# Attention and a two-layer SiLU network on one core: attention sums in sixes and sevens, layer-1 chunks evicted in pairs, and TensorE's order as a table

## The chip, the cores and the metric

The kernel runs on one core of a Trainium2 chip. The metric is the device time of one execution in microseconds (us). The engines are called by the profile's names: PE is TensorE (PEld its weight loads), DVE is VectorE, ACT is ScalarE, POOL is GpSimd, SP is SyncE.

## The reference

```python
# q, k, v: [8 batches, 8 heads, 576 positions, 64], x 0.1
scores = q @ k.T / 8                              # per batch and head
mask_plain = (rel >= 0) & (rel < 32)              # heads 0 to 3, rel = query - key
mask_dil = (rel >= 0) & (rel < 128) & (rel % 4 == 0)   # heads 4 to 7
attn = softmax(where(mask, scores, -1e9)) @ v
x = attn.transpose(0, 2, 1, 3).reshape(4608, 512)
h = x @ w_in                                      # [512, 2048]
out = (h * sigmoid(h)) @ w_out                    # [2048, 512], float32
```

## The kernel before

**Attention, batch by batch.** The four plain heads are cut into six blocks of 96 queries (`QB`), each with 128 keys. The four dilated heads are cut by residue (position modulo 4, `DIL`) into four sequences of 144, and each of these into two halves of 72 (`MH`). A batch goes through these steps: for batches 0 to 2, transposes of k and q on PE (`TA`, `TB`, `TS` plain; `TD`, `TR` dilated), for batches 3 to 7 DMA transposes instead; `S`, six or seven score tiles, with an exponential on ACT (L701 and L705) and, behind batch 0, a mask product on DVE (L711); `V`, a copy of the dilated values (`vd_of`); `P` and `D`, the attention sums (`av`, L735); `XP` and `XD`, transposes of the sums into the input `xA` of layer 1 (batches 0 to 4; batches 5 to 7, `BYDMA`, store to DRAM in `x_s` and come back by DMA transposes).

In `av` four matmuls, one per head, each write 65 columns of one PSUM bank: 64 sums and, in the last, the sum of the weights. DVE then takes the reciprocal of the four weight sums (L741) and multiplies (L742) into `oP` or `oD`. There are six `P` and eight `D` steps in a batch, 14 in all, with 4 x 64 columns each.

**The two layers, by groups of tokens.** `GROUPS` are two groups of 256 tokens (0 and 1) and eight of 512 (2 to 9). Layer 1 (`l1`, L970) makes one chunk of 128 hidden columns with four matmuls into a bank `h`. ACT applies SiLU directly (L984), or, while its tables are those of the exponential, Tanh into `th` (L987), after which DVE finishes with `(th + 1) * h` (L989); both write `gT`. Groups 8 and 9 (`FAST1`, `l1_fast`, L1077 onwards) multiply by the scheme of Strassen and Winograd with seven products of half size. Layer 2 is plain for groups 0 and 1 (L1129) and uses seven products for groups 2 to 9 (`layer2_fast`, L1209), in two blocks a group. It needs sums of `gT` blocks (`g_sums`, L1165, on DVE; group 8 on POOL). Its results leave PSUM by ACT (L1229, L1239) and DVE (L1236) into `ob`, and the store of `ob` is issued on ACT's queue, from group 7 on SP's. `ob` has two buffers.

**PSUM.** Eight banks: `h` two, `y` and `u` for layer 2, `x` and `z` for attention's small tiles and, in groups 0, 1, 8 and 9, for layer 1, and two for scores (`s`). Scores can also take the pairs `hh` or `xz`.

**What sets the order.** The kernel writes each engine's instructions out itself. A planner (`Plan`) holds a clock, the time at which each engine is free, and estimated costs. Each piece of work is a `Step` whose generator issues its matmuls first and then says which engine it uses for how long; `ANY` lets the planner choose ACT or DVE by which would end first. At every turn the loop at the end of the kernel makes a list of candidates, from the attention steps `att` (at most `LOOK` ahead), layer 1 (`l1`, in order, or `LOOK1` ahead in groups 8 and 9), layer 2 (`l2`) and the block sums (`sums`), and starts the first that is ready in planned time and whose engine has no more than a limit of backlog:

```python
cands = main + cands if side > SIDE else cands + main
...
    r = max(r, plan.t + plan.backlog(it[1].uses) - lim)
    if r <= plan.t:
        pick = q_, it
```

The order within attention is the list `order` in `attention(b)`, one for batch 0, one for batches 1 and 2, one for the rest. On the chip each engine works through its own list in order and waits on semaphores, and nothing of the planner's clock remains.

Of the kernel before, what the change touches and what calls it, by code (L numbers as in the profile page):

```python
# [10 lines left out]
F32 = mybir.dt.float32  # L11
# [5 lines left out]
def kernel(  # L17
# [43 lines left out]
    LOOK1 = 6  # L61
# [36 lines left out]
    oD = cpool.tile([MH, 2, DIL, HN, D], F16, name="oD")  # L98
    rcps = cpool.tile([P, NB + 2 * DIL, HN], F32, name="rcps")
# [166 lines left out]
    for t in probs:  # L266
        c = 2 * 4 * MH
        n = PW + P - c
        nc.scalar.copy(t[:, c:], vraws[1].rearrange("p a h r d -> p (a h r d)")[:, :n])
# [46 lines left out]
    HOP = 0.18  # L316
# [3 lines left out]
    LEAN = 0.1  # L320
    ORD = 1

    class Step:
        def __init__(self, make, pe, rings=(), deps=(), uses=()):
            self.make, self.pe, self.rings, self.deps, self.uses = make, pe, rings, deps, uses
            self.after = self.keep = self.done = self.mate = self.behind = None
            self.started = False
            self.freed = None
            self.mode = 128

    class Plan:
# [13 lines left out]
        def push(self, step, gen, ready, value=None):  # L345
            self.now = ready
            try:
# [3 lines left out]
                return  # L351
            heapq.heappush(self.heap, (ready, self.n, step, gen, eng, us))
            self.n += 1

        def flush(self):
            while self.heap and self.heap[0][0] <= self.t:
# [9 lines left out]
                if eng in ("EXP", "L1", "SILU"):  # L366
                    mode = "silu" if eng == "SILU" else "exp"
                    if eng == "L1" and (self.table == "silu" or not self.soon()):
                        mode = "silu"
                    if mode == "silu" or eng == "EXP":  # L370
# [3 lines left out]
                if eng == "ANY":  # L374
                    ends = {e: max(ready, self.free[e]) + n for e, n in us.items()}
                    eng = min(ends, key=ends.get)
# [153 lines left out]
    def attention(b):  # L530
# [204 lines left out]
        def av(ring, key, o, rcp, lhs, rhs):  # L735
            a = small(ring, [P, HN, 66], F32, f"av_{b}_{key}")
            for i in range(HN):
                nc.tensor.matmul(a[:, i, : D + 1], lhs(i), rhs(i), start=True, stop=True)  # L738
            n = o.shape[0]
            yield "DVE", 0.545  # L740
            nc.vector.reciprocal(rcp[:n], a[:n, :, D : D + 1])  # L741
            nc.vector.tensor_tensor(  # L742
                o, a[:n, :, :D], rcp[:n, :, None].broadcast_to([n, HN, D]), ALU.mult
            )

        def av_p(ring, j):
            def lhs(i):
                return prob_cols(("p", j, i // 2), i % 2)

            yield from av(  # L750
                ring, f"p{j}", oP[:, j], rcps[:, j], lhs, lambda i: vp[:, i * NB + j, : D + 1]
            )
            parts[j // 3] += 1
            if b in BYDMA and parts[j // 3] == 3:
                j = j // 3 * 3
# [7 lines left out]
                x_stored(b, j // 3)  # L763

        def av_d(ring, ab, r):
            def lhs(i):
                return prob_cols(("d", ab, r // 2, i), r % 2)

            yield from av(
                ring, f"d{ab}{r}", oD[:, ab, r], rcps[:, NB + ab * DIL + r], lhs,  # L770
                lambda i: vd[:, ab, i, r, : D + 1],
            )
            parts[2 + ab] += 1
            if b in BYDMA and parts[2 + ab] == DIL:
                r0 = BYDMA.index(b) * S + ab * DIL * MH
                rows = x_s[r0 : r0 + DIL * MH, HN * D :].rearrange("(m r) c -> m r c", r=DIL)
                nc.sync.dma_start(out=rows, in_=oD[:, ab].rearrange("p r h d -> p r (h d)"))
                yield "DMA", 3.0
                x_stored(b, ab)
# [32 lines left out]
        if b == 0:  # L812
            order = [
                ("TA", 1, "q"), ("TA", 0, "q"), ("V", 0), ("TD", 3), ("TS", 1), ("TS", 0),
                ("TD", 0), ("TA", 0, "k"), ("TD", 2), ("TD", 1), ("TA", 1, "k"), ("S", 3),
                ("TR",), ("S", 4), ("S", 6), ("S", 0), ("S", 1), ("D", 0, 1), ("P", 1), ("S", 5),
                ("D", 0, 0), ("D", 0, 2), ("V", 1), ("P", 0), ("S", 2), ("P", 3), ("P", 2),
                ("D", 1, 1), ("P", 4), ("D", 0, 3), ("P", 5), ("XP", 0), ("XP", 1), ("D", 1, 2),
                ("XD", 0), ("D", 1, 0), ("XP", 4), ("D", 1, 3), ("XP", 5), ("XP", 2), ("XD", 1),
                ("XP", 3), ("M",), ("B",),  # L820
            ]
        elif b < ORD:
            order = [
                ("N", "k"), ("TD", 3), ("TD", 0), ("TD", 2), ("V", 0), ("TD", 1), ("N", "rest"),
                ("TA", 1), ("N", "q"), ("S", 3), ("TA", 0), ("TB", 0), ("TB", 1), ("D", 0, 1),
                ("D", 0, 0), ("S", 4), ("D", 0, 2), ("S", 0), ("P", 1), ("S", 1), ("D", 0, 3),
                ("P", 2), ("P", 0), ("XP", 0), ("XP", 1), ("S", 5), ("S", 6), ("XD", 0), ("V", 1),
                ("D", 1, 3), ("XP", 2), ("S", 2), ("D", 1, 2), ("D", 1, 0), ("D", 1, 1), ("P", 3),
                ("XP", 3), ("P", 4), ("XD", 1), ("P", 5), ("XP", 4), ("XP", 5),
            ]  # L830
        elif pe_path:
            order = [
                ("N", "k"), ("TD", 3), ("TD", 0), ("TD", 2), ("V", 0), ("TD", 1), ("N", "rest"),
                ("TA", 1), ("N", "q"), ("TA", 0), ("TB", 0), ("TB", 1), ("S", 3), ("S", 4),
                ("S", 0), ("S", 1), ("S", 5), ("S", 6), ("S", 2), ("D", 0, 1),
                ("D", 0, 0), ("D", 0, 2), ("P", 1), ("D", 0, 3),
                ("P", 2), ("P", 0), ("XP", 0), ("XP", 1), ("XD", 0), ("V", 1),
                ("D", 1, 3), ("XP", 2), ("D", 1, 2), ("D", 1, 0), ("D", 1, 1), ("P", 3),
                ("XP", 3), ("P", 4), ("XD", 1), ("P", 5), ("XP", 4), ("XP", 5),
            ]  # L840
        else:
            order = [
                ("S", 0), ("S", 1), ("S", 2), ("S", 3), ("S", 4), ("S", 5), ("P", 1), ("P", 0),
                ("V", 0), ("P", 2), ("D", 0, 0), ("XP", 0), ("V", 1), ("D", 0, 1), ("XP", 1), ("D", 0, 2),
                ("D", 0, 3), ("XP", 2), ("P", 3), ("P", 4), ("XD", 0), ("P", 5), ("D", 1, 0),
                ("XP", 3), ("D", 1, 1), ("XP", 4), ("D", 1, 2), ("D", 1, 3), ("XP", 5), ("XD", 1),
# [3 lines left out]
        for key in order:  # L850
            kind, a = key[0], key[1:]
            rings = ["x", "z"] + (["h", "y", "u"] if b == 0 else ["h"] if b < 2 else [])
# [48 lines left out]
            elif kind == "P":  # L901
                us = sorted({home["p", a[0], hp][0] for hp in range(HP // 2)})
                st = Step(
                    lambda ring, a=a: av_p(ring, *a), 0.13, rings,
                    [AT_VP1 if b == 0 and a[0] > 2 else at_vp] + [steps["S", u] for u in us],
                    ("DVE",),
                )
            elif kind == "D":
                us = sorted({home["d", a[0], a[1] // 2, h][0] for h in range(HN)})
                st = Step(  # L910
                    lambda ring, a=a: av_d(ring, *a), 0.13, rings,
                    [steps["V", a[0]]] + [steps["S", u] for u in us], ("DVE",),
                )
            elif kind == "XP":
                st = Step(lambda ring, a=a: x_p(ring, *a), 0.1, rings, [steps["P", a[0]]], x_eng)
            else:
                st = Step(
                    lambda ring, a=a: x_d(ring, *a), 0.28, rings,
                    [steps["D", a[0], r] for r in range(DIL)], x_eng,
# [16 lines left out]
            if kind in "PD":  # L936
# [3 lines left out]
                if 3 <= b + 2 < B:  # L940
                    st.after = lambda: count(
                        ("V", b), NB + 2 * DIL,
# [24 lines left out]
    def layer1(g, deps):  # L967
        w = GROUPS[g][1]

# [27 lines left out]
        queue, even, odd = [], [], []  # L997
# [421 lines left out]
```

## Time and profile before

| | |
|---|---|
| runs shown | 303.99, 305.06, 305.07 us, median 305.06 |
| profiled execution | 305.17 us, its span in the profile 303.4 us |
| granted TensorE clock | 0.989 of full speed, at half from about 7.5 to 14.3 us |
| PE, DVE, ACT, POOL busy | 288.5, 215.2, 194.6, 97.9 us |
| layer 1 (L975), layer 2 (L1209), groups 8 and 9 (L1077), plain layer 2 (L1129) | 27%, 27%, 8%, 4% of the chain that ended last |

The shares of busy time are averages over stages with different limits: attention of batches 0 to 2 with its transposes lies before about 80 us, layers 1 and 2 with the attention of batches 3 to 7 from there to 230 us, and the seven-product layers alone behind that. Rows of the windows give busy times by stage, rows of the timeline give start and length and, in brackets, how long the engine had been idle and what released it. A matmul's row reaches to the modelled end of its results, while the next matmul can start before that.

### The profile page before, as it was taken

How to read it: one execution, taken by the hardware profiler on the slowest of the kernel's cores; microseconds unless marked ns; L12 is line 12 of the kernel's file. 1: busy time of each engine (PE TensorE's matmuls, PEld its weight loads, DVE VectorE, ACT ScalarE, POOL GpSimd, SP SyncE). 2: the span in 40 equal slices, each digit the busy share in tenths (PEclk: the TensorE clock that was granted, in tenths of full speed). 3: DMA queues.
4: the chain of work that ended last, by engine and by line, in shares of the span. 5: the costliest groups of instructions: out<-in, count | busy, mean ns of one | idle time of the engine just before them, and what ended most of it. 6: DMA issues, size and time to landing. Idle time of an engine off the chain costs nothing.

```text
span 303.4 us, 7434 instructions
## 1 busy us (share of the span) xinstructions
PE 288.5 (95%) x2922; PEld 203.0 (67%) x2922; DVE 215.2 (71%) x598; ACT 194.6 (64%) x427; POOL 97.9 (32%) x135
## 2 busy tenths in 40 slices
PE   6779999989999999999989999999999999999995
PEld 2458765644567666666765577558647888888884
DVE  6288999889958785768654788476767686599511
ACT  7477784378687766766746675667665496388320
POOL 8764824000740060005000659700700069800000
PEclk9599999999999999999999999999999999999999
DMA  7999999999899989989958999943114401200231
GB/s 97 180 199 198 197 194 201 208 186 194 94 155 171 240 101 182 214 179 118 210 128 182 158 192 264 211 84 110 47 34 108 110 2 50 90 2 0 86 124 71
DMA packets 100106, 42.26 MB, mean 139 GB/s; under 512 B 68584, under 2 KB 95464, under 8 KB 100072
## 3 DMA queue, kind: packets, MB, share of 16 engines
q0 software_dynamic: 48528, 19.86, 54.2%
q1 hardware_dynamic: 48088, 15.64, 26.0%
q10 hardware_dynamic: 3456, 6.29, 6.2%
q8 instruction: 23, 0.38, 0.5%
q14 instruction: 11, 0.09, 0.1%
HBM read 39.81 MB, written 17.10 MB: 188 GB/s over the span
## 4 chain that ended last, share of the span: by engine, by line
PE 77%; DVE 11%; DMA 6%; ACT 3%; issue 1%; POOL 1%; ACTq 0%; DVEq 0%; POOLq 0%
PE h L975 27%; PE y L1209 27%; PE h L1077 8%; PE y L1129 4%; DMA out_dram<-ob 4%; PE av_d L738 2%; PE s L692 2%; DMA nat<-in_q_dram 2%; DVE gT L989 2%; PE av_p L738 1%; DVE probs L711 1%; DVE oD L742 1%; DVE ob L1236 1%; DVE oP L742 1%; PE xp L784 1%
## 5 line engine op out<-in xcount | busy, mean ns | idle before, releaser
L975 PE MATMUL h<-xA,w_in 128*128 128x512 f16 (+1 forms) x512 | 110.4, 352 | 1.8 <-ACT probs L705 0.9
L984 ACT ACTIVATE gT<-h 128x512 f16<-128x512 f32 x84 | 49.6, 597 | 29.0 <-PE h L975 28.6
L975 PEld LDWEIGHTS <-w_in 128*128 128x128 f16 x512 | 45.2, 97 | 32.6 <-issue 2.5
L1209 PEld LDWEIGHTS <-gT 128*128 128x128 f16 x512 | 49.0, 98 | 8.6 <-issue 1.6
L1209 PE MATMUL y<-w_out,gT 128*128 128x256 f16 x384 | 48.4, 273 | 0.1
L1209 PEld LDWEIGHTS <-work 128*128 128x128 f16 x384 | 37.0, 98 | 7.0 <-issue 1.1
L1236 DVE TENSOR_TENSOR ob<-y,nat 128x256 f32<-128x256 f32 x48 | 20.1, 422 | 25.4 <-PE y L1209 23.3
L512 POOL COPY fence<-kqT 128x1 f16<-128x1 f16 x10 | 3.9, 397 | 94.8 <-DMA kqT<-kq_s 94.8
L1209 PE MATMUL y<-w_sum,work 128*128 128x256 f16 x256 | 32.0, 273 | 0.4 <-ACT nat L1229 0.4
L738 PEld LDWEIGHTS <-probs 128*128 128x128 f16 x448 | 22.9, 98 | 13.0 <-DVE oP L742 1.7
L701 ACT ACTIVATE probs<-s 128x768 f16<-128x768 f32 (+2 forms) x31 | 24.5, 791 | 6.3 <-PE s L692 3.4
L742 DVE TENSOR_TENSOR oD<-av_d,rcps 72x256 f16<-72x256 f32 x64 | 26.9, 421 | 2.2
L1229 ACT COPY nat<-y 128x256 f32<-128x256 f32 x48 | 17.9, 384 | 10.7 <-PE y L1209 9.5
L987 ACT ACTIVATE th<-h 128x256 f32<-128x256 f32 (+1 forms) x44 | 19.2, 445 | 7.3 <-PE h L975 4.7
L989 DVE SCALAR_TENSOR_TENSOR gT<-th,h 128x256 f16<-128x256 f32 (+1 forms) x44 | 20.6, 487 | 2.2 <-ACT th L987 2.1
L741 DVE RECIPROCAL rcps<-av_d 72x4 f32<-72x4 f32 x64 | 11.1, 173 | 14.9 <-PE av_d L738 14.8
L1239 ACT COPY ob<-y 128x256 f32<-128x256 f32 x16 | 5.9, 371 | 24.2 <-PE y L1209 21.6
L705 ACT ACTIVATE probs<-s 128x288 f16<-128x288 f32 (+2 forms) x40 | 18.5, 485 | 4.6 <-ACT ob L1239 1.4
L742 DVE TENSOR_TENSOR oP<-av_p,rcps 96x256 f16<-96x256 f32 x48 | 20.2, 421 | 1.6
L711 DVE TENSOR_TENSOR probs<-probs,mask_p 128x768 f16<-128x768 f16 x21 | 12.2, 584 | 10.2 <-ACT probs L701 7.4
L1209 PE MATMUL y<-w_sum,gT 128*128 128x256 f16 x128 | 16.6, 272 | 1.0 <-DVE ob L1236 1.0
L738 PE MATMUL av_d<-vd,probs 128*128 128x65 f16 x256 | 16.5, 194 | 0.6 <-ACT probs L705 0.3
(129 smaller groups left out, 484.3 us busy)
## 6 DMA issues: line engine op xcount, KB each, us to landing
out_dram<-ob ACTq DMA_DIRECT2D x24, 256.0 KB, 4.0
out_dram<-ob SPq DMA_DIRECT2D x12, 256.0 KB, 2.0
kq_s<-in_k_dram POOLq DMA_DIRECT2D x5, 576.0 KB, 9.1
kq_s<-in_q_dram POOLq DMA_DIRECT2D x5, 576.0 KB, 12.9
vp<-in_v_dram POOLq DMA_DIRECT2D x7, 384.0 KB, 7.0
w_out<-in_moe_w_out_dram POOLq DMA_DIRECT2D x4, 512.0 KB, 10.9
vraw<-in_v_dram POOLq DMA_DIRECT2D x8, 224.0 KB, 5.4
w_in<-in_moe_w_in_dram POOLq DMA_DIRECT2D x3, 512.0 KB, 9.5
```

What stands on the lines that cost most here:

```text
L701: nc.scalar.activation(p2, both[:, :, :n], AF.Exp, scale=scale)
L705: nc.scalar.activation(p2[:, i], sp[i][:, :n], AF.Exp, scale=scale)
L738: nc.tensor.matmul(a[:, i, : D + 1], lhs(i), rhs(i), start=True, stop=True)
L742: nc.vector.tensor_tensor(o, a[:n, :, :D], rcp[:n, :, None].broadcast_to([n, HN, D]), ALU.mult)
L975: nc.tensor.matmul(h[:, :w], w_in16[:, c, f * P : (f + 1) * P], x_g[:, c], start=(c == 0), stop=(c == HP - 1),)
L984: nc.scalar.activation(gTs[g][:, f, :w], h[:, :w], AF.Silu, scale=2.0)
L987: nc.scalar.activation(th[:, :w], h[:, :w], AF.Tanh)
L989: nc.vector.scalar_tensor_tensor(gTs[g][:, f, :w], th[:, :w], 1.0, h[:, :w], ALU.add, ALU.mult)
L1077: nc.tensor.matmul(y, lhs[:, c, j], rhs[:, c], start=first and c == 0, stop=c == 1, skip_group_check=not first,)
L1209: nc.tensor.matmul(y, lhs[:, c, tb * P : (tb + 1) * P], rhs[:, c], start=first and c == 0, stop=c == KP - 1, skip_group_check=not first,)
L1229: nc.scalar.copy((t1, t5, u2)[n], y)
L1236: nc.vector.tensor_tensor(half, y, (u2, t5, t1)[n - 3], ALU.add)
```

## The change

It has three parts.

1. **Attention sums.** The 24 plain sums of a batch (6 blocks x 4 heads) and the 32 dilated sums (2 halves x 4 residues x 4 heads) are counted through in one row each. `RUN_P` and `RUN_D` cut them into runs of six, and of seven, seven, six, six and six, and each run fills one bank of up to 7 x 66 columns with one reciprocal and one multiply. `P` has four steps, `D` five. `XP` j waits for the runs that hold its four sums, `XD` for three runs; a run can span two blocks or both halves.
2. **Layer 1 of groups 0 and 1.** `l1_two` makes two chunks of 256 columns in one bank and evicts both with one SiLU, or one Tanh and one product.
3. **The order.** The candidates loop is replaced by a table: `SEQ` names, start by start, the queue (`a` attention, `l` layer 1, `y` layer 2, `s` sums) and the place in it. Steps without matmuls start as soon as their inputs are there in planned time (`early`). `CHOICE` fixes the engine of some copies and SiLU or Tanh for some chunks, and `SHIFT` moves the planned time of some steps, which changes where their instructions stand on ACT and DVE. `HOP` goes from 0.18 to 0.16 and `LEAN` from 0.1 to 0.05, `FAST1`'s look-ahead `LOOK1` is gone, the lists `order` are rewritten for the new steps, and sums of batch 0 no longer take the bank `y`. `keep_warm` is defined, but the table has no `w`. The eight copies that fill the ends of `probs` run from the last buffer to the first.

```diff
+    RUN_P = (0, 6, 12, 18, 24)
+    RUN_D = (0, 7, 14, 20, 26, 32)
...
-    HOP = 0.18
+    HOP = 0.16
...
-    LEAN = 0.1
+    LEAN = 0.05
...
+            ready += shift.get(f"{step.name}.{step.n}", 0.0)
...
-                    eng = min(ends, key=ends.get)
+                    eng = choice.get(f"{step.name}.{step.n}") or min(ends, key=ends.get)
...
+        def av(ring, kind, t, o, at, unit):
+            n0, n1 = (RUN_P, RUN_D)[kind == "d"][t : t + 2]
+            a = small(ring, [P, 7, 66], F32, f"av_{b}_{kind}{t}")
+            for n in range(n0, n1):
+                blk, i, rhs = unit(n)
+                nc.tensor.matmul(
+                    a[:, n - n0, : D + 1], prob_cols(blk, i), rhs, start=True, stop=True
+                )
+            yield "DVE", 0.275 + (n1 - n0) * D / 960
+            rows = o.shape[0]
+            rcp = rcps.rearrange("p n i -> p (n i)")[:rows, at + n0 : at + n1]
+            got = a[:rows, : n1 - n0]
+            nc.vector.reciprocal(rcp[:, :, None], got[:, :, D : D + 1])
             nc.vector.tensor_tensor(
-                o, a[:n, :, :D], rcp[:n, :, None].broadcast_to([n, HN, D]), ALU.mult
+                o[:, n0:n1], got[:, :, :D], rcp[:, :, None].broadcast_to([rows, n1 - n0, D]), ALU.mult
             )
...
-            rings = ["x", "z"] + (["h", "y", "u"] if b == 0 else ["h"] if b < 2 else [])
+            rings = ["x", "z"] + (["h", "u"] if b == 0 else ["h"] if b < 2 else [])
...
+        def l1_two(ring, f):
+            gT_of(g)
+            h = POOLS[ring].tile([P, 2, w], F32, tag=ring, name=f"h_{g}_{f}")
+            x_g = x_of(g)
+            for n in range(2):
+                for c in range(HP):
+                    nc.tensor.matmul(
+                        h[:, n], w_in16[:, c, (f + n) * P : (f + n + 1) * P], x_g[:, c],
+                        start=(c == 0), stop=(c == HP - 1),
+                    )
+            mode = yield "L1", 0.11 + 2 * w / 1200
+            gT = gTs[g][:, f : f + 2, :w]
+            if mode == "silu":
+                nc.scalar.activation(gT, h, AF.Silu, scale=2.0)
+                return
+            th = o32.tile([P, 2, w], F32, tag="th", name=f"th_{g}_{f}")
+            nc.scalar.activation(th, h, AF.Tanh)
+            yield "DVE", 0.12 + 2 * w / 960
+            nc.vector.scalar_tensor_tensor(gT, th, 1.0, h, ALU.add, ALU.mult)
...
+    SEQ = (
+        "aI aG aD aG aH aF aF aB aA aE aA aE aE aG aC aA aI aA aD aB aC aC aA aF aA aA aM aA aB "
...
+    todo = SEQ.split()
+    early = []
+    while todo or plan.heap or early:
...
+        if todo:
+            q_, i = queues[todo[0][0]], CODE.index(todo[0][1])
+            st = q_[i][1]
+            r = plan.ready(st)
+            if not st.pe or r is not None and r <= plan.t:
+                todo.pop(0)
+                q_.pop(i)
+                if st.pe:
+                    plan.start(st)
+                else:
+                    early.append(st)
                 continue
```

## The prediction

> **What bounds the kernel now.** I read the page first (busy shares, chain), then the windows by stage, then the timeline where TensorE (PE) stood still.
>
> ```profile
> span 303.4 us, 7434 instructions
> PE 288.5 (95%) x2922; PEld 203.0 (67%) x2922; DVE 215.2 (71%) x598; ACT 194.6 (64%) x427; POOL 97.9 (32%) x135
> PE 77%; DVE 11%; DMA 6%; ACT 3%; issue 1%; POOL 1%; ACTq 0%; DVEq 0%; POOLq 0%
> ```
>
> TensorE sets the time: 95% busy and 77% of the chain of waits. VectorE (DVE) is next on the chain with 11%. The windows say where (columns: window, length, then busy us and count of PE, PEld, DVE, ACT, POOL; granted clock; DMA share; GB/s):
>
> ```profile
> 0.00:10.10 10.10, 5.13 (x34) 2.17 (x34) 5.27 (x21) 6.41 (x12) 8.39 (x17) 0.87 1.00 117
> 10.10:23.00 12.90, 11.17 (x192) 7.19 (x193) 8.03 (x29) 9.19 (x25) 8.94 (x13) 0.84 1.50 192
> 23.00:60.00 37.00, 36.34 (x396) 25.22 (x396) 33.74 (x99) 23.18 (x59) 14.53 (x19) 1.00 1.49 199
> 60.00:80.00 20.00, 18.33 (x200) 9.87 (x198) 17.89 (x46) 15.51 (x30) 2.49 (x5) 1.00 0.96 162
> 80.00:145.00 65.00, 64.69 (x663) 42.48 (x661) 47.59 (x133) 46.35 (x95) 16.01 (x23) 1.00 1.24 169
> 281.00:303.40 22.40, 18.71 (x172) 16.52 (x169) 6.60 (x17) 5.13 (x14) 0.00 (x0) 1.00 0.26 95
> ```
>
> From 10.1 to 80 us DVE is busy 59.7 of 69.9 us, and there PE is idle for 4.1 us. Idle understates the loss: eight layer-2 matmuls make a row of 1.04 us but are issued in 8 x 0.109 = 0.87, so a wait under 0.17 hides in the row's tail. I therefore took every matmul's start in the timeline, and subtracted the median spacing of its shape. The shortfall is 4.3 us before 10.1, then 4.2 (to 23), 3.65 (to 60), 4.5 (to 80), 7.8 (80 to 230) and 0.7 after: 25.1 in all. Part of it is fixed: each change between the 64-row score matmuls and the others costs 0.116 on average (66 of them behind 10.1 us, 7.7 us). Without those, 3.1 + 1.9 + 3.35 = 8.3 us of waits lie between 10.1 and 80, and 4.2 between 80 and 230. These are what the change can win; PE's own work is the same 2922 matmuls of the same shapes.
>
> What such a wait looks like:
>
> ```profile
> 64.75 0.10 PEld L975 LDWEIGHTS <-w_in 128*128 128x128 f16 x1
> ...
> 65.84 1.02 PE L975 MATMUL h<-xA,w_in 128*128 128x512 f16 x4 [0.89 <-ACT probs L705]
> ```
>
> The weights are in at 64.85, the matmul starts a microsecond later: every bank is held by something that ACT and DVE have not emptied.
>
> **The change, part by part.** Its own time is the profiled execution's 305.17 us, span 303.4 plus 1.77 around it; the median of the runs is 305.06, so 0.1 comes off at the end.
>
> *Fewer, larger evictions of attention sums.*
>
> ```profile
> L742 DVE TENSOR_TENSOR oD<-av_d,rcps 72x256 f16<-72x256 f32 x64 | 26.9, 421 | 2.2
> L741 DVE RECIPROCAL rcps<-av_d 72x4 f32<-72x4 f32 x64 | 11.1, 173 | 14.9 <-PE av_d L738 14.8
> L989 DVE SCALAR_TENSOR_TENSOR gT<-th,h 128x256 f16<-128x256 f32 x32 | 12.4, 414 | 1.6 <-ACT th L987 1.5
> L989 DVE SCALAR_TENSOR_TENSOR gT<-th,h 128x512 f16<-128x512 f32 x12 | 8.2, 680 | 0.6 <-ACT th L987 0.6
> ```
>
> A reciprocal and its multiply take 0.545 from pair to pair (starts 20.25 and 20.80). The two L989 rows give 266 ns for 256 more elements, 1.04 ns each, so a pair of six sums costs 0.545 + 0.133 = 0.68 and one of seven 0.745. A batch had 14 pairs, 7.63 us; it gets seven sixes and two sevens, 6.25. That is 1.4 us of DVE per batch, 11 in all, but worth something only where DVE is late: batches 0, 1 and 2. Against it, one eviction answers 0.13 to 0.2 us later, and a transpose of outputs (XP, XD) waits for one or two larger units instead of exact ones.
>
> *Two layer-1 chunks per eviction in groups 0 and 1.* All 32 chunks go by Tanh and the L989 product, with ACT at 384 ns and DVE at 414 each. Sixteen pairs at 607 (the 512-wide Tanh) and 680 save 2.6 us of ACT and 2.4 of DVE. The first chunk of a pair waits one chunk longer, 4 x 0.109 = 0.44. Cover: four banks rotate (h twice, x, z), so three more pairs of 0.87, 2.6 us, are issued before a bank comes back; its way out is about 0.25 + 0.61 + 0.68 and two hand-overs of 0.1, 1.75 us. Hidden at nothing; if attention holds x and z, the cover is 0.87 and each pair could wait 0.9.
>
> [...]
>
> *Fewer Tanh routes in group 2* (seven 512-wide become four): DVE loses 3 x 0.68 = 2.0 us in the 60 to 80 stage. Together DVE is relieved by 3 x 1.38 + 2.4 + 2.0 = 8.5 of its 59.7 us there.
>
> *The written order, head.* The first plain transposes are of k instead of q. Today PE stands 2.22 us until q lands at 10.12 and then does q and k; a load of k had landed by 9.19, where a POOL issue that waited for it starts. The 16 k transposes (0.64 on the chain) move into the wait: -0.65. If k is late with q, nothing.
>
> *10 to 23 us* (batch 0). DVE is 1.4 us shorter, and waits are 3.1; but the longer single evictions stand directly before XP with little to fill in. Bounds: -3.1 and +0.8 (six such places at 0.13). I take -1.2. *23 to 60*: waits 1.9, relief of 3.8 on DVE; bounds -1.9 and +1, I take -1.0. *60 to 80*: waits 3.35, relief 3.4, DVE 17.89 of 20 busy; bounds -3.35 and 0, as the relief is as large as the waits. I take -2.2, and two mode changes fewer, -0.2.
>
> *80 to 230 us.* The written order cuts the score bursts of batches 4 to 7 into more pieces: 36 changes of mode instead of 24, +12 x 0.116 = +1.4. Waits there are single ones; the longest is for an output buffer still being stored:
>
> ```profile
> 155.57 0.42 DVE L1236 TENSOR_TENSOR ob<-y,nat 128x256 f32<-128x256 f32 x1 [1.19 <-DMA out_dram<-ob]
> 156.05 1.03 PE L1209 MATMUL y<-w_sum,gT 128*128 128x256 f16 x8 [0.95 <-DVE ob L1236]
> ```
>
> The store was issued at 148.26 and held it 7.2 us. In today's order three blocks of layer 2 have only 5.1 to 5.9 us of matmuls between filling a buffer and refilling it while scores run (second blocks of groups 3, 4, 5). The new order makes these 13 or more, but makes three others 5.0 to 6.1 (first blocks of 4, 5, 6). The same count, so only -0.8 of the 4.2; bounds -2.8 and +2.
>
> *Queues.* POOL's instructions keep their order up to group 8's sums. On SP a store of oP of batch 5 now stands ahead of both plain transposes of batch 6; it waits for four sums that the order finishes early. Table loads of ACT stay 12. All free here.
>
> *The end.* The last 14 layer-2 products keep their order (281 to 299 us without a gap, then the last store), at no change. Group 9's last layer-1 step is moved behind four of the seven products before them. Behind it queue an add (0.41), a Silu (0.63), two output evictions of DVE and the sums (0.56): the first sum is ready 3.1 us later, by the evictions, and is needed 4.5 products of 0.875 later, 3.9. Hidden with 0.8 to spare.
>
> Sum: -0.65 - 1.2 - 1.0 - 2.4 + 1.4 - 0.8 = -4.65; 305.17 - 4.65 - 0.1 = **300.4 us**. About 0.5% (1.5 us) is what a measurement of this kernel can tell from no change.
>
> **The rivals.** *Cut bursts (slower).* In batches 4 to 7 each extra piece of scores not only pays its two mode changes but finds its bank not yet emptied by the exponentials, as in the row where PE starts one score matmul at 149.36 and the next eleven at 149.74 (0.37 lost), or 0.58 at 181.2. Six extra pieces at 0.5 are 3.0, with the 1.4 +4.4; with the gains before 80 us at half (-2.6) the time is 305.17 + 1.8 - 0.1 = 306.9. It decides (1.5 us slower) as soon as the gains before 80 us are below 2.9. For it: 78 mode changes instead of 68 stand in the order. Against it: layer-2 products lie between the pieces, which give ACT 0.87 us and more each. [...]
>
> *Paired chunks stall.* If attention holds x and z while group 1 runs, eight pairs wait 0.45 (half of 0.9): +3.6 in place of -1.0, 305.0. For it: attention of batch 1 is spread through group 1. Against it: attention's own matmuls are cover too.
>
> *The relief doesn't reach PE.* The waits before 80 us are then ACT's (15.5 of 20 busy from 60 to 80) and only the head and the mode changes remain: 305.17 - 0.65 + 1.2 - 0.1 = 305.6.
>
> **How the numbers follow.** The forecast has 0.68 (0.66 faster, 0.02 same), cut bursts 0.18 (0.02 same, 0.16 slower), paired chunks 0.09 (0.04, 0.04, 0.01), no relief 0.05 (0.02 same, 0.03 slower). Faster 0.70, same 0.10, slower 0.20. Low end: all 8.3 us of waits up to 80 go, with the head, half of the 4.2 less 1.4, and 0.2: -9.85, 295.2. High end: the cut bursts with a little more, 307. About 0.05 lies below and 0.1 above. Of the likeliest case alone: 296 to 303.
>
> **What would show it.** Right: DVE clearly below 59 us between 10 and 80, its evictions of sums at 0.68 to 0.75 per pair, 72 reciprocals; PE's idle from 60 to 80 below 0.8 us; the first k transposes before 10 us; the end unchanged. Wrong: PE waits on scores or on ob between 120 and 230 above 5 us, xp rows with idle for oP above 0.4 us in batch 0, or h rows of groups 0 and 1 waiting for the product.

## The result, and the profile after

The changed kernel takes 306.09 us (median of 20 runs, 304.68 to 312.21), the kernel before 304.52 in as many runs beside it (303.53 to 305.82). The ratio is 1.0055, 95% interval 1.0034 to 1.0076: slower by half a per cent, where 300.4 was forecast. The runs of the kernel before lie within 2.3 us, those of the changed one within 7.5. Ratios here leave out runs that lie far above the fastest of the same kernel; as some kernels below are thrown back by a wait of their own in most runs, the median and the extremes of all runs stand beside each ratio.

The page of the profiled execution (305.41 us, span 303.5):

```profile
span 303.5 us, 7297 instructions
PE 288.0 (95%) x2922; PEld 203.4 (67%) x2922; DVE 208.2 (69%) x508; ACT 193.0 (64%) x406; POOL 97.9 (32%) x135
PE 75%; DMA 15%; DVE 4%; ACT 2%; POOL 1%; issue 1%; ACTq 0%; DVEq 0%; POOLq 0%
```

VectorE has lost 7 us of work and most of its place on the chain (11% to 4%), and DMA has taken that place (6% to 15%). The span is where it was. The windows by stage:

```profile
10.10:23.00 12.90, 11.25 (x194) 7.30 (x193) 7.80 (x23) 9.32 (x23) 8.94 (x13) 1.00 1.48 194
23.00:60.00 37.00, 34.94 (x408) 25.07 (x408) 31.53 (x71) 22.21 (x45) 14.63 (x20) 1.00 1.48 196
60.00:80.00 20.00, 18.88 (x205) 10.35 (x202) 17.34 (x41) 15.13 (x30) 2.25 (x5) 1.00 1.00 168
162.00:200.00 38.00, 35.77 (x340) 23.67 (x339) 23.31 (x52) 22.90 (x41) 22.32 (x31) 1.00 1.21 188
281.00:303.50 22.50, 18.87 (x173) 16.66 (x171) 6.90 (x17) 5.76 (x15) 0.00 (x0) 1.00 0.26 95
```

The same window of the kernel before, late in the program:

```profile
162.00:200.00 38.00, 37.46 (x348) 23.65 (x346) 27.55 (x72) 24.02 (x43) 22.61 (x31) 1.00 1.13 198
```

From 60 to 80 us PE is busier by 0.55 us, and from 162 to 200 idler by 1.7, in a stretch where the prediction had added no wait. The groups show that the evictions became what was said, and that the paired chunks do not stall PE (0.3 us of idle in front of 128 matmuls):

```profile
L756 DVE TENSOR_TENSOR oD<-av_d,rcps 72x384 f16<-72x384 f32 (+1 forms) x40 | 23.2, 580 | 1.4
L755 DVE RECIPROCAL rcps<-av_d 72x6 f32<-72x6 f32 (+1 forms) x40 | 7.6, 191 | 12.4 <-PE av_d L748 12.3
L986 PE MATMUL h<-xA,w_in 128*128 128x256 f16 x128 | 16.2, 273 | 0.3 <-DMA w_in<-in_moe_w_in_dram 0.2
```

The loss at 176 us, in the timeline (the second row is the issue of a store of output rows, as is the fourth):

```profile
169.70 0.80 POOL L187 DMA_DIRECT2D kq_s<-in_q_dram  x1
170.08 0.34 ACTq L1280 DMA_DIRECT2D out_dram<-ob  x1
...
170.71 6.64 POOL L1065 TENSOR_TENSOR nat<-w_in 128x256 f16<-128x256 f16 x8 [0.21 <-PE s L700]
170.92 0.34 ACTq L1280 DMA_DIRECT2D out_dram<-ob  x1
170.96 0.89 DVE L580 COPY vd<-vraw 128x1024 f16<-128x1024 f16 x1
...
172.93 0.55 DVE L756 TENSOR_TENSOR oP<-av_p,rcps 96x384 f16<-96x384 f32 x1
...
177.83 0.42 DVE L1275 TENSOR_TENSOR ob<-y,nat 128x256 f32<-128x256 f32 x1 [2.88 <-DMA out_dram<-ob]
...
178.30 0.27 PE L1248 MATMUL y<-w_out,gT 128*128 128x256 f16 x1 [1.85 <-DVE ob L1275]
```

Two things are to be seen. The stores of two output rows are issued at 170.08 and 170.92. VectorE, which refills the two buffers in the same order, waits for the first until 177.83 (7.75 us), with a mask product queued behind; PE waits for VectorE. The second store lands after 8.23 us, at 179.15 (`170.92 8.23 DMA out_dram<-ob` in the chain), and holds VectorE for 0.33 us more. And at 170.71 GpSimd begins `wa_sums`, 32 sums of `w_in` for groups 8 and 9, of which 24 run back to back until 187.97; the copy beside them takes 0.89 us where 0.42 is usual. In this execution that holds up nothing that shows, as VectorE then waits 2.88 us for the store anyway. In the kernel before this burst of scores came some 6 us later. The DMA view from 165 to 185 us shows what the store runs beside; after:

```profile
q0 software_dynamic: 5071, 1.97, 99.0%
...
out_dram<-ob ACTq DMA_DIRECT2D x4, 256.0 KB, 8.2
```

and before:

```profile
q0 software_dynamic: 5063, 1.96, 84.0%
...
out_dram<-ob ACTq DMA_DIRECT2D x2, 256.0 KB, 5.8
```

GpSimd's queue q0 carries the loads of batch 7, some 1.97 MB in either kernel. The new order issues its two stores right behind the last of these loads (169.70, the first row above); two more stores follow at 180.03 and 181.19, behind the wait. The old order issues its two at 178.66 and 179.50, more than 5 us behind its last load (173.17). That the loads make the store slow is read from this and was not tried by itself. The times to landing, 8.2 and 5.8, are each that of the one store whose landing the trace holds.

### The profile page after: what moved, and what is told of

Same layout as the page of the kernel before. It is cut to its first block, busy times and chain, and to the rows that moved or that the text cites. A ratio compares the mean times of both kernels' runs of the same rounds, so it can differ in the third digit from the quotient of the medians.

```text
span 303.5 us, 7297 instructions
## 1 busy us (share of the span) xinstructions
PE 288.0 (95%) x2922; PEld 203.4 (67%) x2922; DVE 208.2 (69%) x508; ACT 193.0 (64%) x406; POOL 97.9 (32%) x135
## 4 chain that ended last, share of the span: by engine, by line
PE 75%; DMA 15%; DVE 4%; ACT 2%; POOL 1%; issue 1%; ACTq 0%; DVEq 0%; POOLq 0%
PE y L1248 30%; PE h L1005 25%; PE h L1116 8%; DMA nat<-in_k_dram 6%; PE y L1168 4%; DMA w_out<-in_moe_w_out_dram 4%; DMA out_dram<-ob 3%; DMA w_in<-in_moe_w_in_dram 2%; PE s L700 2%; PE av_d L748 2%; PE av_p L748 2%; DVE gT L1019 1%; DVE probs L719 1%; PE h L986 1%; PE xp L800 1%
## 5 line engine op out<-in xcount | busy, mean ns | idle before, releaser
L1005 PE MATMUL h<-xA,w_in 128*128 128x512 f16 x384 | 93.3, 379 | 0.0
L1005 PEld LDWEIGHTS <-w_in 128*128 128x128 f16 x384 | 33.9, 97 | 30.5
L709 ACT ACTIVATE probs<-s 128x768 f16<-128x768 f32 (+2 forms) x29 | 22.6, 778 | 6.2 <-PE s L700 4.6
L756 DVE TENSOR_TENSOR oD<-av_d,rcps 72x384 f16<-72x384 f32 (+1 forms) x40 | 23.2, 580 | 1.4
L713 ACT ACTIVATE probs<-s 128x384 f16<-128x384 f32 (+2 forms) x44 | 19.6, 477 | 4.0 <-PE s L700 2.7
L756 DVE TENSOR_TENSOR oP<-av_p,rcps 96x384 f16<-96x384 f32 x32 | 17.7, 554 | 1.1
L1248 PE MATMUL y<-w_out,work 128*128 128x256 f16 x128 | 16.6, 272 | 0.1
L986 PE MATMUL h<-xA,w_in 128*128 128x256 f16 x128 | 16.2, 273 | 0.3 <-DMA w_in<-in_moe_w_in_dram 0.2
L1168 PE MATMUL y<-w_out,gT 128*128 128x512 f16 x64 | 16.2, 379 | 0.1
L755 DVE RECIPROCAL rcps<-av_d 72x6 f32<-72x6 f32 (+1 forms) x40 | 7.6, 191 | 12.4 <-PE av_d L748 12.3
```

What stands on the lines that cost most here:

```text
L709: nc.scalar.activation(p2, both[:, :, :n], AF.Exp, scale=scale)
L713: nc.scalar.activation(p2[:, i], sp[i][:, :n], AF.Exp, scale=scale)
L756: nc.vector.tensor_tensor(o[:, n0:n1], got[:, :, :D], rcp[:, :, None].broadcast_to([rows, n1 - n0, D]), ALU.mult)
L986: nc.tensor.matmul(h[:, n], w_in16[:, c, (f + n) * P : (f + n + 1) * P], x_g[:, c], start=(c == 0), stop=(c == HP - 1),)
L1005: nc.tensor.matmul(h[:, :w], w_in16[:, c, f * P : (f + 1) * P], x_g[:, c], start=(c == 0), stop=(c == HP - 1),)
L1168: nc.tensor.matmul(y, gTs[g][:, f, tb * P : (tb + 1) * P], w_out16[:, f], start=(f == 0), stop=(f == NFF - 1),)
```

## The experiments

The first four expectations were written with only the waits of the profile in view; there theory A is the output buffer, B the loads before 57 us and C the cut bursts. From the third experiment on theory A is that VectorE is shut out by GpSimd's sums, theory B that it waits for the stores of `ob`; the rivals are that the new units or the new order are bad in themselves.

**A third output buffer.**

```diff
-            ob = o32.tile([P, DM], F32, tag="ob", name=f"ob_{g}_{tb}")
+            ob = o32.tile([P, DM], F32, tag="ob", bufs=3, name=f"ob_{g}_{tb}")
```

(the same in `layer2_fast`.) On the changed kernel:

> The changed kernel with three output buffers instead of two, every engine's order the same. Theory A (the new order pays at the output buffer: in its profile PE loses 2.6 us at 176 to 179 us, waiting for a store issued at 170.92 that takes 8.2 us, and this wait differs from run to run): 303.0 to 303.7, the runs within 1.5 us of each other, and no wait of PE for DVE ob. Theory B (the loads before 57 us set the time and its spread): 305 to 306 with the same wide spread, since nothing changes before 57 us. Theory C (the bursts cut into more pieces): the waits of PE around scores stay, 305.5.

On the kernel before:

> The kernel before with three output buffers, every order the same. Theory A: its waits for stores (0.95 at 155, 0.3 at 184.6 and half of the 0.58 at 181) go, 303.3 to 303.8, so about 1 us; it stays level with the changed kernel with three buffers or a little above it. Theories B and C: no or little change, 304.3.

Measured: 304.18 us (303.14 to 311.92; ratio to before 0.9990, 0.9964 to 1.0017), and 303.75 (303.13 to 304.89; 0.9976, 0.9959 to 0.9994). The buffer removes the deficit of the changed kernel and gives a little to the old one, but the changed kernel stays above the 303.0 to 303.7 that was expected, and 306.91, 311.85 and 311.92 are among its 12 runs. The profiled execution is one of these (311.85):

```profile
170.23 10.33 DVE L580 COPY vd<-vraw 128x1024 f16<-128x1024 f16 x1
180.49 0.54 DVE L719 TENSOR_TENSOR probs<-probs,mask_p 128x768 f16<-128x768 f16 x1
```

```profile
170.24 5.04 POOL L1065 TENSOR_TENSOR nat<-w_in 128x256 f16<-128x256 f16 x8
175.25 5.03 POOL L1065 TENSOR_TENSOR nat<-nat,w_in 128x256 f16<-128x256 f16 x8
```

```profile
181.78 0.54 PE L700 MATMUL s<-kqT 64*128 64x72 f16 x12 [6.36 <-DVE oP L756]
```

A copy of 0.42 us ends just behind the 16th sum (180.28 us), 10.3 us after it began, and PE stands for 6.36 us. The granted clock then is at half from 180.20 to 187.03 us.

**Parts of the change under the candidates loop of before** (HOP 0.18, LEAN 0.1, no table). Only the shared banks:

> Only the attention sums in sixes and sevens, single chunks in groups 0 and 1, old candidates loop. From the prediction's terms -1.2 in batch 0 and some -0.7 each in batches 1 and 2: 302 to 303. Theory B: 303.5 to 304.5, since DVE relief before 57 us is worth nothing. The difference to the run with paired chunks is what the pairs give: -1.0 by the prediction, 0 by theory B.

Shared banks and paired chunks:

> Attention sums in sixes and sevens and paired chunks, but the order from the old candidates loop with the old constants. Theory A (order of the table places three blocks of layer 2 too close together): the parts keep their gain, 302.0 to 303.5. Theory B (loads hold PE up to 57 us whatever DVE does): only batch 2 gains, 303.0 to 304.3. If the larger units themselves cost more than they save, 305 or more.

Measured: 322.1 us (312.47 to 323.23) and 322.04 (309.9 to 323.79), far above all that was expected. Each program has two levels: 312.5 to 313.8 in three runs and 322.0 to 323.2 in five; 309.9 and 311.2 in two and 321.9 to 323.8 in four. The medians lie some 17.6 us above before (304.4 beside them), the lower levels 5.5 to 9.4 us (ratios 1.0262 and 1.0188). The second program was profiled on its lower level (311.22 us): no VectorE row there is longer than 1.25 us, and PE waits 1.49 us at 181.6 us for VectorE. In the profiled execution of the first (322.25 us) VectorE is shut out for longer still:

```profile
173.82 16.06 DVE L718 TENSOR_TENSOR probs<-probs,mask_p 128x768 f16<-128x768 f16 x3
```

```profile
191.30 1.87 PE L1247 MATMUL y<-w_out,gT 128*128 128x256 f16 x8 [11.11 <-DVE ob L1274]
```

Its 24 sums on GpSimd ran from 173.46 to 188.5 us; of the three products in the row above, the first alone took 15.12 us.

**The sums left out, or later.** In the first kernel `wa_sums` issues nothing; in the others a one-column copy of `oP` stands ahead of it, so that it starts when batch 7's second run is written:

```diff
     def wa_sums(j):
         S1, S2, S3, S4 = wa_sum
+        if j == 0:
+            nc.gpsimd.tensor_copy(fence[:QB, 2:3], oP[:, 2, HN - 1, D - 1 :])
```

All other engines keep their instructions in the same order as in the kernel that is edited.

> Leaves out the 32 sums of w_in that GpSimd makes for groups 8 and 9, so these groups work with stale data; all other engines issue the same instructions in the same order as the changed kernel. Theory A (GpSimd's stream of sums holds up VectorE's float16 copies and mask products of batch 6, and TensorE waits behind them): no row vd<-vraw or probs<-probs,mask above 0.75 us between 165 and 190 us, the largest TensorE wait there below 1.5 us, median 302.0 to 304.0, and no single run more than 2.5 us above the fastest (the changed kernel: 304.7 to 312.2). Theory B (the stall at 176 us is only the late store of ob, and the spread comes from elsewhere): the same median as the changed kernel within 0.7 us, 305.4 to 306.8, and single runs still up to 310 or more.

> The whole computation; GpSimd's 32 sums begin only when batch 7's second pooled output run has been written (a one-column copy from oP stands ahead of them), some 212 us instead of 171, where VectorE has no mask product and no vd copy left. Theory A: as without the sums, 302.0 to 304.5 and single runs within 2.5 us of the fastest; the sums end before 240 us, where TensorE first reads them. Theory B: 305.4 to 306.8 as the changed kernel. A third outcome, slower than the changed kernel, would mean that the sums then hold up the sums of gT on VectorE (L1204) or arrive too late for TensorE at 240 us.

> As the kernel with the late sums, and with a third buffer for the output rows ob, so that VectorE does not wait for the store of 8.2 us that was under way at 176 us. Theory A with the two waits separate: 2.0 us less than late sums alone at most (2.03 + 0.55 us of waits were put down to that store), 300.5 to 303.0. If the store was late only because of what GpSimd's sums did: the same time as with late sums alone within 0.7 us.

> The shared banks and paired chunks under the loop of before (322.0 us median, single runs 309.9 to 323.8), with GpSimd's sums made late in the same way. Theory A: the 16 us between this kernel and before are the lock on VectorE (16.06 us in one row group were seen), so 304 to 308 and single runs within 3 us. Rival C (the old loop simply finds a worse order with the new units): 318 to 324, as without it.

Measured: 308.87 (308.71 to 309.05; 1.0159, 1.0134 to 1.0184), 314.39 (313.39 to 315.07), 311.3 (310.3 to 313.31) and 315.51 (313.56 to 317.34). The third and the fourth missed what was expected of them, the fourth by falling between its two forecasts. Theory A alone falls with the first: without the sums no VectorE row is long, and the kernel is slower. What is left is theory B, larger than before:

```profile
171.30 0.42 DVE L580 COPY vd<-vraw 128x1024 f16<-128x1024 f16 x1
...
179.57 0.42 DVE L1271 TENSOR_TENSOR ob<-y,nat 128x256 f32<-128x256 f32 x1 [4.57 <-DMA out_dram<-ob]
```

Its store took 9.64 us to land against 8.23, and PE's wait grew by as much, from 1.85 to 3.26 us. Behind the longer wait the granted clock falls to half for 3.41 us; the same stretch of this kernel and of the changed one:

```profile
181.66:185.07 3.41, 3.41 (x19) 1.88 (x18) 1.35 (x4) 1.45 (x2) 0.00 (x0) 0.50 1.21 251
181.66:185.07 3.41, 3.41 (x39) 2.26 (x38) 1.76 (x6) 2.75 (x5) 3.41 (x7) 1.00 1.44 280
```

Half of 3.41 us is 1.7; with the 1.4 of the wait that is 3.1 of the 3.3 us between the two profiled executions (308.74 and 305.41). Why the store is slower without the sums stays open. The late sums show that theory A's mechanism is real, by moving it. It was the third outcome written down:

```profile
224.84 9.41 DVE L1207 TENSOR_TENSOR work<-gT 128x1024 f16<-128x1024 f16 x1
```

```profile
228.66 5.04 POOL L1068 TENSOR_TENSOR kqT<-w_in 128x256 f16<-128x256 f16 x8
```

```profile
237.38 1.86 PE L1251 MATMUL y<-w_sum,gT 128*128 128x256 f16 x8 [5.01 <-DVE ob L1278]
```

A sum of gT that takes 0.68 us elsewhere waits until GpSimd's stream is over. With the third buffer (311.3) PE's wait at 178 us shrinks from 2.10 to 0.85 us, and the one behind the sum of gT stays (4.97 us).

**Both causes at once.** The third buffer, with the sums left out:

> The changed kernel with a third output buffer and without GpSimd's 32 sums (groups 8 and 9 work with stale data). Theory A+B (two separate costs near 176 us: the output store of 8 to 10 us that holds VectorE through two buffers, 2.6 to 4.0 us; and the sums that shut out VectorE, 0 to 6 us by chance): with both gone the median is 301.5 to 303.5, no wait of TensorE above 1.2 us after 80 us, and single runs within 1.5 us of the fastest. If something else still costs the changed kernel its gain: 304 or more.

> The kernel before with a third output buffer and without GpSimd's 32 sums. It showed neither cost in size (303.75 with the buffer alone): 303.0 to 304.0. The difference to the changed kernel in the same state is what the change itself is worth: by theory A+B 0.5 to 2 us in favour of the changed kernel, since its TensorE was 1.8 us ahead at 160 us. Rival D: no difference within 0.5 us, so the change saves nothing that reaches the end.

With the third buffer and the sums on VectorE:

```diff
-            yield "POOL", 0.2 + 4 * P / 480
-            for c in range(2):
-                nc.gpsimd.tensor_tensor(
-                    o[:, c, j : j + 2], a[:, c, j : j + 2], b[:, c, j : j + 2], op
-                )
+            yield "DVE", 0.15 + 4 * P / 1920
+            nc.vector.tensor_tensor(o[:, :, j : j + 2], a[:, :, j : j + 2], b[:, :, j : j + 2], op)
```

> The changed kernel, whole, with a third output buffer, and the sums of w_in on VectorE (16 instructions of 128 x 512 at some 0.41 us, 6.6 us in all, behind batch 7's scores) and none on GpSimd. Theory A: no VectorE row is shut out, so 302 to 304.5 and single runs within 2 us, up to 1.5 us of it TensorE waiting behind the added 6.6 us near 212 us. If the order on VectorE there is tight: 305 to 307 with a wait of TensorE of 2 to 4 us near 212 us.

> The kernel before with the same two edits, as the control of the run above: 303.0 to 305.0; by theory A slower than the changed kernel with these edits by 0.5 to 2 us, by rival D the same within 0.5 us.

Measured: 303.98 (302.32 to 308.31; 0.9979, 0.9956 to 1.0001), 303.18 (302.77 to 304.94; 0.9957), 309.35 (306.41 to 312.23) and 306.82 (306.25 to 307.18). Both theories together expected 303.5 or less of the first, and less than of the kernel before with the same edits; it is 0.8 us above that. Its trace has the reason:

```profile
178.29 0.75 DVE L1271 TENSOR_TENSOR ob<-y,nat 128x256 f32<-128x256 f32 x2 [2.12 <-DMA out_dram<-ob]
```

Three buffers are still too few: the store is still awaited, and PE stands for 1.33 us behind it. Beside the run with the sums in their place (304.18) the sums cost 0.2 us at the median, so with three buffers their cost is in single runs. On VectorE the sums only move the wait: PE stands for 2.12 us at 217.4 us, beside 2.47 at the store, and both kernels are slower than was expected. The control is not a clean one, as the loop of before reacts to the load that is planned for VectorE and also moves matmuls from 214 us on.

**Five buffers.** Output rows and tanh rows, both 2 KB, share one ring of five (`tag="o5", bufs=5` at all places), in place of two and two. Without the sums; and with the sums in two halves, each behind a copy of `oP`:

> The changed kernel without GpSimd's 32 sums (groups 8 and 9 work with stale data) and with five buffers that output rows and tanh rows share, in place of two and two. Theory B' (what is left at 177 us with three buffers, 1.49 us, is still VectorE waiting for the stores of ob that lie among batch 7's loads): no VectorE wait on out_dram<-ob of over 0.5 us between 160 and 200 us, no wait of TensorE over 1 us behind 80 us, median 301.3 to 302.8, and the runs within 1.5 us of each other. Rival E (TensorE waits there for the mask products or the exps themselves): a wait of 1 to 2 us stays near 177 us and the median is 303.5 to 304.5 as with three buffers.

> The changed kernel, whole, with the five shared buffers, and GpSimd's sums in two halves: 16 from batch 6's second pooled output run on (some 181 us, when the mask products and copies of batch 6 are done) and 16 from batch 7's on (some 213 us). Theory A+B': 301.5 to 303.5, no VectorE row between float16 SBUF tiles above 1.5 us, which beats both kernels. If the halves meet VectorE's sums of gT after all (213 to 215 us, 223 us): a row of several us there, and 304 to 308.

> The kernel before with the same two edits, as the control. It had neither wait in size, so 303.0 to 304.5. Theory A+B': 1 to 2 us slower than the changed kernel with them; rival D (the change itself is worth nothing): the same within 0.5 us.

And the new units under the old loop, without the sums:

> The shared banks and paired chunks under the loop of before, without GpSimd's 32 sums (groups 8 and 9 work with stale data): 322.0 us with the sums where they were, 315.5 with late sums. Theory A: the most of the 17 us over before is VectorE shut out by the sums, so 304 to 309, and runs within 3 us. Rival C (the old loop's order with the new units is bad in itself): 315 or more.

Measured: 302.59 (301.45 to 304.11; 0.9938, 0.9915 to 0.9961): theory B holds, no wait of PE above 0.8 us is left behind 40 us, and rival E is out. From 162 to 200 us PE has no idle at all:

```profile
162.00:200.00 38.00, 38.00 (x365) 25.65 (x362) 23.19 (x54) 24.78 (x45) 4.84 (x7) 1.00 1.19 188
```

The ring also serves the Tanh rows of the first 80 us, and the executions with it lose some 0.5 us less (changed) and 0.9 less (before) from 23 to 60 us than those without; so part of what five buffers give may not be the store's. Five buffers with the sums left in their place were not run. The halves took 310.0 (308.32 to 310.43) and 306.87 (301.84 to 308.86): in the changed kernel the first copy read batch 7's run, so that all sums ran from 208 to 229 us and a sum of gT took 9.54 us from 219.98 on. It was not the test it was meant to be. In the kernel before the halves came apart, but the second met a sum of gT (4.41 us from 221.38 on), and PE waited 2.78 us. The old loop without the sums takes 307.85 (307.26 to 311.53; 1.0129): of the 17.6 us over before at the upper level some 14 go with the sums, and some 2 to 4 at the lower one. Of the other 3 us, PE's wait behind a store at 180 us is 1.60; the rest was not taken apart.

**The sums in VectorE's gaps.** Five buffers; 16 sums behind batch 6's first dilated run, 16 behind batch 7's scores:

```diff
         S1, S2, S3, S4 = wa_sum
+        if j == 0:
+            nc.gpsimd.tensor_copy(fence[:MH, 2:3], oD[:, 0, 0, 0, D - 1 :])
         for o, a, b, op in (
             (S1, A21, A22, ALU.add), (S2, S1, A11, ALU.subtract),
-            (S4, A12, S2, ALU.subtract), (S3, A11, A21, ALU.subtract),
+            (S3, A11, A21, ALU.subtract), (S4, A12, S2, ALU.subtract),
```

> The changed kernel, whole, with the five shared buffers, and with GpSimd's sums moved into two gaps of VectorE's work between float16 SBUF tiles: 16 from batch 6's first dilated output run on (some 181 to 191 us; the first 1024-wide sum of gT came at 192.5 us) and 16 behind batch 7's scores (some 207 to 217 us; the next 1024-wide sum at 223 us). Theory A+B': both waits are gone as in the run without sums (302.59), so 301.5 to 303.5, no such VectorE row above 1.5 us, single runs within 2 us; faster than both kernels. If a float16 row meets the stream after all: a row of 5 to 10 us, and 305 to 310.

> The kernel before with the same two edits. Its first dilated output of batch 6 comes later (some 188 us), so the first 16 sums run to 198 us, over the 1024-wide sums of gT at 197 us: theory A allows a wait of up to 1.5 us there, 303.0 to 305.0. Rival D (the change is worth nothing by itself): the changed kernel with these edits within 0.5 us of this one; theory A+B': the changed one faster by 1 us or more.

Measured: **301.71 us** (301.45 to 303.09; 0.9913, 0.9887 to 0.9938) and 303.47 (302.74 to 303.81; 0.9958, 0.9939 to 0.9976). The first beats both kernels. Its page and its window:

```profile
span 299.9 us, 7292 instructions
PE 288.0 (96%) x2922; PEld 203.3 (68%) x2922; DVE 207.1 (69%) x508; ACT 193.0 (64%) x406; POOL 96.0 (32%) x136
```

```profile
162.00:200.00 38.00, 38.00 (x363) 25.61 (x362) 23.63 (x56) 24.80 (x45) 15.00 (x24) 1.00 1.17 194
```

PE has no idle from 162 to 200 us; the longest VectorE row between float16 tiles is 1.22 us. With the same two edits on both sides the change is worth 303.47 - 301.71 = 1.8 us. In the kernel before the first sums still meet a sum of gT (1.77 us at 194.27), behind which PE waits 0.54 us, so some of the 1.8 may be that.

## Why the prediction was wrong

The shortfall of PE by stage, worked out as in the prediction (start to start, against the median spacing of each shape in the trace of before). The means are over the profiled executions in each of the two orders; no edit of the experiments is aimed at a stage ahead of 162 us. In the last two rows the pair stands instead, the two kernels with the sums in the gaps.

| stage, us | forecast | before, after | means of 6 and 10, or the pair |
|---|---|---|---|
| to 10.1 | -0.65 | 4.26, 4.18 | 4.01, 3.50 |
| 10.1 to 23 | -1.2 | 4.19, 4.06 | 4.18, 4.87 |
| 23 to 60 | -1.0 | 3.65, 4.75 | 3.57, 4.05 |
| 60 to 80 | -2.4 | 4.48, 2.73 | 4.58, 2.67 |
| 80 to 162 | +0.6, with the next | 5.04, 4.09 | 3.86, 4.09 |
| 162 to 200 | | 1.93, 3.83 | 1.85, 1.60 |
| behind 200 | 0 | 1.54, 1.60 | 1.86, 1.35 |

- **Head, 60 to 80 us, end: right.** The head gained 0.5 of 0.65 on average (hardly in the profiled pair, where PE stood 2.43 us until 7.9 us for a load of q, and the first k transposes began at 10.03 instead of before 10 us). From 60 to 80 us 1.9 of 2.4 came. PE's idle there is 1.12 us, not below 0.8. The order of the end cost nothing.
- **The durations: right.** 580 and 191 ns a pair are 0.69 us from start to start for six sums and 0.77 for seven (0.68 and 0.745 forecast), 72 pairs. But VectorE fell only from 59.7 to 56.7 us between 10 and 80, not by 8.5: the evictions gave 3.5 and the products 3.6, while copies that went to VectorE added 1.3 and sums of gT that now came ahead of 80 us 1.4 (rows overlap, so the groups do not add up to the 3.0). The sum took the written choices of engines at nothing.
- **10 to 60 us: wrong, 2.2 forecast to be won and 1.2 lost.** In each of the ten executions the two stages together lose more than in any of the six. Part of it is the bound that was named: outputs wait for a larger unit. In the timeline of after:

```profile
21.31 0.21 PE L816 MATMUL xd<-ident_w,oD 72*128 72x72 f16 x1 [0.29 <-DVE oD L756]
22.00 0.26 PE L800 MATMUL xp<-ident_w,oP 96*128 96x96 f16 x2 [0.30 <-DVE oP L756]
...
30.68 0.37 PE L612 MATMUL td<-ident_w,nat 96*128 96x96 f16 x5 [0.88 <-DMA nat<-in_q_dram]
40.37 0.37 PE L748 MATMUL av_d<-vd,probs 128*128 128x65 f16 x7 [0.69 <-DVE vd L580]
```

  More comes at two fixed places of the table: it asks for a transpose of batch 1 at 29.8 us, before its load has landed, and for an attention sum at 39.7 before the `vd` copy. The relief of VectorE cannot pay where a load is last: the chain of after runs through loads up to 43.9 us. This is read from the traces and was not tried by an edit, so the cause of this miss stays open.
- **80 to 230 us: the step that failed.** It counted tight places of the output buffer by the matmuls between filling and refilling, found three in either order, and took -0.8 of bounds from -2.8 to +2. It set no duration for the store in the new place, though its own row had one of 7.2 us. The wait at 178 us is at one of the three places that it named, the first block of group 4. There a store takes 7.75 us and more, and the 6 us of matmuls do not cover it: PE lost 1.85 us in the profiled execution and more in others (3.26 without the sums). With five buffers the wait is gone. At the other two places (first blocks of groups 5 and 6) no such wait stands in the profiled execution.
- **What the sum did not have at all:** GpSimd's sums. The prediction passed the POOL queue as "instructions keep their order" and free. They start when batch 6's scores are done, which the new order brings forward from 176.5 to 170.7 us, on top of VectorE's copy and mask products. They can cost 6.36 us of PE's idle (the profiled execution with three buffers; with the half clock behind it the shortfall from 162 to 200 us is 10.48, against 3.08 without the sums), but not in every run.
- **The mode changes: right.** From 80 to 162 us 22 instead of 18 cost 2.63 instead of 1.87, from 162 to 200 14 instead of 6 cost 1.46 instead of 0.94 (the pair with the sums in the gaps): +1.3 of the +1.4.
- **The rivals.** "Cut bursts" gave 306.9, near the result, but by another mechanism: no score matmul of after waits as described, and without the two waits above the order is faster than before. "Paired chunks stall" is out by the row of L986: 0.3 us of idle in front of 128 matmuls.

So of the 4.65 us 1.8 are there once both waits are gone; the head and the 60 to 80 us stage give it, with 0.5 behind 200 us that was not forecast, and 10 to 60 us take some of it back. The 2.9 us that are missing from the 4.65 are the 3.4 between forecast and outcome from 10 to 60 us, less what came out better elsewhere. That the change came out slower and not faster is the two waits, as is shown by taking them away together; what each costs by itself is shown only in part (the third buffer alone brings the changed kernel from 306.09 to 304.18 us, in separate sets of runs).

## What to carry to other kernels

A written order fixes where every engine stands when a transfer runs, so each wait that an order moves must be priced with the DMA load of the place that it comes to: a store of 256 KB took 5.8 us when issued more than 5 us behind the last of a batch's loads (before), and 8.2 (after) and 9.6 (after without the sums) right behind it, and a buffer count that sufficed before did not after. GpSimd's stream of sums was no free cover beside VectorE's work between SBUF tiles (SBUF is the memory on the core that holds the tiles): a copy of 0.42 us took 10.33 beside it, and PE stood for 6.36 us. Start such a stream by a condition (here a one-column copy) in a gap of VectorE's rows: with that and five buffers the longest such row was 1.22 us, and the kernel took 301.71. And when a kernel's runs scatter more than those of the kernel before, one profile is not enough: the row of 10.33 us did not stand in the changed kernel's own, and did in the next kernel's.

## What the runs showed of the hardware

**VectorE beside GpSimd.** VectorE rows between float16 SBUF tiles that take 0.42 to 0.68 us elsewhere lasted 10.33 us (the third buffer), 15.12 (shared banks under the old loop), 9.41 (the late sums) and 9.54 and 4.41 (the halves, on the changed kernel and on the one before) beside back-to-back GpSimd sums. Each ended 0.3 to 0.6 us behind the last sum before GpSimd paused, though each GpSimd instruction lasts 0.63 us (a mean over eight). Eight sums beside such a row took 5.04 us, as they do beside evictions from PSUM alone (5.05). In other runs the same rows only stretched (0.42 to 0.89 us, 0.55 to 1.02), and there the sums stretched too (6.64 us for eight). Evictions from PSUM beside the same stream kept their 0.55 us (172.93 us in after). Which of the two happens was not settled by an edit; the order of instructions is the same. What holds the rows up was not shown either.

**The clock behind a long wait.** In the kernel without the sums, behind PE's wait of 3.26 us, the granted clock was 0.50 for 3.41 us; in the changed kernel, behind one of 1.85 us, it was 1.00 in the same window. With the third buffer it was at half for 6.83 us (180.20 to 187.03), with PE standing for 6.36 us until 181.78. With the late sums the slices of the page at 179 to 187 and at 234 to 241 us have a clock of 0.7; PE's waits there are 2.10 and 5.01 us, and behind the second the rows of eight layer-2 matmuls at 237.38 and 239.04 us took 1.86 and 1.83 us, where 1.04 is usual. With the late sums and the third buffer the waits are 0.85 and 4.97 us, and only the second has such a slice (0.7, at 232 to 239 us). Length alone does not decide it: behind a wait of 2.47 us (the sums on VectorE) such a row took 1.03 us (178.49). So a wait like these can cost some 1.7 us more than its idle time (an estimate, half of 3.41).
